# A gated attention kernel: chunks 1 to 5 in halves of 64 tokens, with one matmul for scores x v and q x state

## The chip, the core and the metric

The kernel runs on one core of a Trainium2 chip. A core has five engines that matter here, each with its own queue that it works off in order: TensorE (PE; its weight loads are listed as PEld), VectorE (DVE), ScalarE (ACT), GpSimd (POOL) and SyncE (SP), which issues nearly all transfers between device memory and the on-chip memory. TensorE writes its results to PSUM, from where ScalarE or VectorE fetch them. The metric is the device time of one execution in microseconds (us); lower is better.

## The reference

Two parts follow one another. The first is a gated linear attention, for 4 batches, 8 heads, 768 tokens and 48 features a head. It keeps a 48 x 48 state for each head:

```python
for t in range(S):
    state = alpha[:, :, t, :, None] * state + np.einsum('bhd,bhe->bhde', k[:, :, t], v[:, :, t])
    y[:, :, t] = np.einsum('bhd,bhde->bhe', q[:, :, t], state)
```

Its output is laid out as 4 x 768 rows of 384 values. The second part normalizes each row, multiplies it by a gain and sends it through two layers with a ReLU between them:

```python
xn = (x - mu) / np.sqrt(var + 1e-06) * g_ln
ch = np.maximum(xn @ w_ch1, 0.0) @ w_ch2
return (x + ch)
```

`w_ch1` is 384 x 1536 and `w_ch2` is 1536 x 384. Both arrive as 64-bit floats; the kernel turns them into 32-bit floats on the core.

## The kernel before

**Tiling.** The tokens are cut into 6 chunks of 128. `attention(c, b)` handles chunk c of batch b with tokens on the partitions: 24 blocks. Inside a chunk the recurrence is written with the running sum L of log alpha. `tri`, a triangle of ones, times log alpha gives L in PSUM (`lps`, line 249). ScalarE makes exp(-L) (`ek`, line 253) and exp(L) (`eq`, 254). GpSimd forms k x exp(-L) (line 256), VectorE q x exp(L) (258). TensorE transposes both (`tps`, 272), and ScalarE or VectorE copies them to `qkT` (276, 278). The scores are k against q, two heads at a time in the upper and lower half of the array (`aps`, 285); VectorE keeps the causal ones in `at` (289). The output `yps` is the sum of q x state (302, not in chunk 0) and scores x v (307). The state for the next chunk is the old one plus k x v (`sps`, 321; 326), times the gate exp(L) of the chunk's last token (331, on GpSimd). The gate goes from the last row of `eq` to a DRAM row (262) and back as columns (294). The output is stored (`kept`, 314), normalized (335 to 342), transposed (349) and copied to `xT` (351).

**The two layers.** `mlp()` takes chunk after chunk, with all four batches as columns. Chunk 0 is done directly (`hidden`, 372, and `project`, 384). Chunks 1 to 5 use a scheme with fewer products of combined blocks: `hidden_product` (612) and `product` (455). It needs sums of blocks of the operands: of w1 (`combine_first`, GpSimd, 565), of w2 (`combine_weights`, GpSimd, 415), of x (`combine_x`, VectorE, 588) and of the hidden values (`combine_hidden`, VectorE, 442). VectorE adds the products up (465, 468, 622 to 655), GpSimd does some late sums (471, 631 to 651), and ScalarE the ReLUs (664). `take_weights(i)` rounds one of 12 pieces of the weights, in three steps on VectorE, ScalarE and VectorE, and then starts the load of a later piece.

**What sets the order.** Every one of these functions yields after a few instructions, and the string `ORDER` says which takes the next turn: the letters a to x are the 24 attention blocks, A to L the pieces of weights, M the two layers, S the sums of the weights, R, X, N and O the ReLUs, sums and output loads. Each engine's queue is filled in the order of these turns.

**PSUM.** The pool has three tags: "a", three slots, for `lps`, `tps` and `aps`; "s", two slots, for `yps`, `sps` and `xps`; "m", three slots, for the two layers.

**Loads.** `load` brings one tensor of one chunk and batch in one transfer of 192 KB, on SP's queue. At the start alpha comes first, then k and q, then v, then three pieces of weights.

Of the kernel before, what the change touches and what calls it, by code (L numbers as in the profile page):

```python
# [25 lines left out]
    "babdabcdcabadcbacabbdabaabacababdabacbdbccbadAccdddcBcCedfeacbacaeBeffcgbaededbe"  # L26
    "eghfbAefgfcachfbdcheaaffbaefgdjBddeedbdcgfbeicCjgdfihcgjdCeAhccAgBDfghddEfeOgegi"
    "DfDeeiMfhMMMiMDMMiegMGEgEMMMOfeGghhigMMjhiCEfggFMhOGFHFgMGghMiHkfMMfiHeFIjhfHeMM"
    "IkJSIhhkhhlMMjIMfMglKJKjJLfgMljjLKLhhMSSMihSikMhOSgiMMSSMgShjkSjhiiMXjiSXSiXiXMk"
    "kMXkSllMXMXMlSMMXnMnMMkSMSMSiXmMSXMnMSMSMSMSjkMMkikjMXlMMMMMMRMllMMMljOMRSMMMSlk"  # L30
    "jlklMjjSRimMMnMSMjRMMMnMMMMkMnnmnMMMkMRMpjMMMnMRlMlllnmMmiRmOlMSmMRmMoMmmOMMJMRM"
    "SmSjmNSjlRMMRmoNinjkkNMmNMMkolMNRpoMlOKpMNMmMMMoMmoNmMNkNMMMNMMNMnMNqMkMNMMMopMM"
    "NSMMnolMoMlNpkNMoMMMOkOMMonnXXXXpMMXXMMXXXpoMMMMMMMMpXMMXMMoMMMrMMMMqMMMrMMMmnMM"
    "pRMomRnprmmMRqRopMMpMRMoMMmRmMMMMMrprnMnrnMMMoopppnMtpMqRMMMOMtrqMqnMMoMpqMprMRq"
    "RMMqNsMqMOMNRMNtrRnrMNMqMqqNMssRMMMNssoMMMNMNNMNsMMMNopMqqqqqrMMNMMsNtpMMNMMOprM"
    "MMNqsMqtMMooMMsNpMMXMMsMXXMstMqrrXtuXXXMtMMXXMMvMMMMXsvMMMtXMstMOrMMMMMMMMMvMMrr"
    "rsMtMvOsMMrtMMMMLuRMsMMvvMMMMMRRMtMrRMuMORvxMMMRRMstrMMstRqttsMqRuMsMMNRMuMRNMMN"
    "NMvMtuurvMxMMMMNsNtRtMMwNNvMMMsrMNMwMMNNMNMMwtNMMuMMuuMMMMMNuMwMNMMNwMMuttsxMMuv"
    "XXXvxMvuuXXXXxvwxMXMxxMMuwMXMwxMMXMMXMMMMMvMMwMwMxMMMRMuOwMuOMMwMMMMwuMMxwMwRMRM"
    "MxRMMRMvMMMMwxMMMMMMMMMuMMuMRMRRvMMMRNwxuRMMvMOMRxMMxvwMMNwMxNNMNxRNMMuxMMwMNMvM"  # L40
    "MONMwMNNMNMMMNwMMNMxMxMMvMMxwNMONMMNxMMMvMMXvOXXXMXXXMMMMMMXXMMMMMMMMXMMMMMRMXMM"
    "RMMMMMMMMMMMMMMMRRMMMMORMMMMMRMMMMRMMMMMMMMMRMRRMRMMNMMMNMMMNNNRMMNNMNMNMMMNNMMM"
    "ONMNMMMMMMMMMMMMMNNMMNMMMMMMM"
# [4 lines left out]
def kernel(  # L48
# [51 lines left out]
    raw = ctx.enter_context(tc.tile_pool(name="raw", bufs=B))  # L100
# [7 lines left out]

    r = np.arange(P)
    upto = (r[None, :] >= r[:, None]).astype(np.float32)  # L110
    const_np = np.concatenate([upto, np.eye(P, dtype=np.float32)], 1)
# [3 lines left out]
    def load(c, b, names="akqv"):  # L115
        for n, src in (("a", alpha), ("k", k), ("q", q), ("v", v)):
            if n not in names:
                continue
            t = raw.tile([P, H, D], FP32, name=f"r{n}", tag=f"r{n}",
                         bufs=B)  # L120
            nc.sync.dma_start(t, src[b, c * P:(c + 1) * P])
            raws[n, c, b] = t
# [5 lines left out]
    for names in ("a", "kq", "v"):  # L128
        for b in range(B):
            load(0, b, names)  # L130
# [4 lines left out]
    g_col, g20 = small[:, :NF], small[:, NF:2 * NF]  # L135
    eps, least = small[:, 2 * NF:2 * NF + 1], small[:, 2 * NF + 1:]
# [6 lines left out]
    for i in range(NJ // 2):  # L143
        cs, js = slice(2 * i * P, 2 * (i + 1) * P), slice(2 * i, 2 * (i + 1))
        pieces.append((w1[:, :, cs], w1_src[:, :, cs], True))
        pieces.append((w2[:, js], w2_src[:, js], False))
# [3 lines left out]
    def load_weights(i):  # L150
        if i >= len(pieces):
            return
        dst, src, _ = pieces[i]
        if src.dtype != FP32:
            dst = staged[i] = stage.tile(list(dst.shape), INT64, name="ws", tag="ws")
        nc.sync.dma_start(dst, src)

    def round_weights(i):
# [4 lines left out]
        dst, _, gains = pieces[i]  # L163
# [14 lines left out]
        if not gains:  # L178
            stt(out=dst, in0=dst, scalar=2.0 ** -20, in1=hi.bitcast(FP32),
                op0=AOP.mult, op1=AOP.mult)  # L180
            return
        for f in range(NF):
            stt(out=dst[:, f], in0=dst[:, f], scalar=g20[:, f:f + 1],
                in1=hi[:, f].bitcast(FP32), op0=AOP.mult, op1=AOP.mult)

    def take_weights(i):
        if pieces[i][1].dtype != FP32:
            yield from round_weights(i)
        elif pieces[i][2]:
            for f in range(NF):  # L190
                nc.vector.tensor_scalar_mul(pieces[i][0][:, f], pieces[i][0][:, f],
                                            g_col[:, f:f + 1])
        yield
        load_weights(i + STAGED)
        yield

    for i in range(STAGED):
        load_weights(i)
# [8 lines left out]
    eqs = [cpool.tile([P, NP, 2, 64], FP32, name=f"eq{b}") for b in range(2)]  # L207
    eqs += [shared[:, i * NP * P:(i + 1) * NP * P].rearrange(
        "p (a b c) -> p a b c", b=2, c=64) for i in range(2)]
    qks = [cpool.tile([P, 2, NP, 2, 64], FP32, name=f"qk{b}") for b in range(3)]  # L210
    qks.append(shared[:, 2 * NP * P:].rearrange("p (i a b c) -> p i a b c", i=2, b=2, c=64))
    sts = [cpool.tile([P, NP, 2, D], FP32, name=f"st{b}") for b in range(B)]
    for b in range(B):
        nc.vector.memset(eqs[b].rearrange("p a b c -> p (a b) c")[:, :, D:], 0.0)
        nc.vector.memset(qks[b].rearrange("p i a b c -> p (i a b) c")[:, :, D:], 0.0)
        nc.gpsimd.memset(sts[b], 0.0)
# [15 lines left out]
    ats = [cpool.tile([P, 2, NP, P], FP32, name=f"at{i}") for i in range(2)]  # L232
# [9 lines left out]
    def attention(c, b):  # L242
        qk = qk_of(c, b).rearrange("p i a b c -> p i (a b) c")
        eq = eq_of(c, b).rearrange("p a b c -> p (a b) c")[:, :, :D]
        la = work.tile([P, H, D], FP32, name="la", tag="la")
# [3 lines left out]
        nc.tensor.matmul(lps[:, :DM], tri, la, start=True, stop=True)  # L249
        yield  # L250
        lv = lps[:, :DM].rearrange("p (h d) -> p h d", d=D)
        ek = work.tile([P, H, D], FP32, name="ek", tag="ek")
        nc.scalar.activation(out=ek, in_=lv, func=AFT.Exp, scale=-1.0)
        nc.scalar.activation(out=eq, in_=lv, func=AFT.Exp)
        yield
        nc.gpsimd.tensor_mul(qk[:, 1, :, :D], raws.pop(("k", c, b)), ek)  # L256
        yield
        nc.vector.tensor_mul(qk[:, 0, :, :D], raws.pop(("q", c, b)), eq)
        if c + 1 < NCB:
            row = dram.tile([1, NP, P], FP32, name="row", tag="row")  # L260
            gate = work.tile([P, NP], FP32, name="gate", tag="gate", bufs=B)
            nc.sync.dma_start(row, eq_of(c, b)[P - 1:P].rearrange("o a b c -> o a (b c)"))
        yield
        n = c * B + b + (B if c < 2 else B // 2)
        if c < 2 or 3 * B <= n < NCB * B:
            load(*divmod(n, B), "akq")
        yield
        qkT = work.tile([R, 2, NP, P], FP32, name="qkT", tag="qkT", bufs=2)
        for i in range(2):
# [5 lines left out]
            if i == 0 or c < 2:  # L275
                nc.scalar.copy(out=qkT[:, i], in_=tps)  # L276
            else:
                nc.vector.tensor_copy(out=qkT[:, i], in_=tps)
            yield
        at = ats[b % len(ats)]  # L280
        aps = [ps.tile([P, NP, P], FP32, name=f"aps{i}", tag="a", bufs=3) for i in range(2)]
        for p in range(NP):
            for i in range(2):
                rows = slice(64 * i, 64 * i + D)
                nc.tensor.matmul(aps[i][:, p], qkT[rows, 1, p], qkT[rows, 0, p],  # L285
                                 start=True, stop=True)
        yield
        for i in range(2):
            nc.vector.copy_predicated(out=at[:, i], data=aps[i],  # L289
                                      mask=mask.unsqueeze(1).broadcast_to([P, NP, P]))  # L290
        yield
        if c + 1 < NCB:
            with nc.allow_non_contiguous_dma(reason="one row to columns"):
                nc.sync.dma_start(gate, row.rearrange("o a c -> c (o a)"))
        yield
        vt = raws.pop(("v", c, b))
        yps = ps.tile([P, NP, 2, D], FP32, name="yps", tag="s")
        sides = [slice(64 * s, 64 * s + 64) for s in range(2)]
        for p in range(NP):
            if c > 0:  # L300
                for s in sides:
                    nc.tensor.matmul(yps[s, p].rearrange("p a b -> p (a b)"), qkT[:, 0, p, s],  # L302
                                     sts[b][:R, p].rearrange("p a b -> p (a b)"),
                                     start=True, stop=False)
            for i in range(2):
                for s in sides:
                    nc.tensor.matmul(yps[s, p, i], at[:, i, p, s], vt[:, 2 * p + i],  # L307
                                     start=(c == 0), stop=(c == 0 or i == 1))
        yield
        x = work.tile([P, DM], FP32, name="x", tag="x", bufs=3)  # L310
        nc.scalar.copy(out=x, in_=yps.rearrange("p a b d -> p (a b d)"))
# [3 lines left out]
        yield  # L315
        if c + 1 < NCB:
            sps = ps.tile([R, NP, D], FP32, name="sps", tag="s")
# [407 lines left out]
```

## Time and profile before

| | |
|---|---|
| median of 3 runs | 476.17 us (473.99 to 476.75) |
| span of the profiled execution | 472.3 us |
| VectorE: scores kept, L289, x48 | 724 ns each |
| VectorE: q x exp(L), L258, x20 | 797 ns each |
| VectorE: copy of the transposed k, L278, x16 | 682 ns each |
| VectorE: normalization, L342, x24 | 587 ns each |
| GpSimd: k x exp(-L), L256, x22 (2 more in another tile) | 1059 ns each |
| GpSimd: state x gate, L331, x20 | 959 ns each |
| ScalarE: copies of the transposed q and k, L276, x32 | 597 ns each |
| ScalarE: exp(-L), L253, x24 | 490 ns each |
| HBM read and written | 33.20 and 9.48 MB |

The profile is of one execution, and its span runs from the first to the last instruction; what lies before and after it is part of the device time alone. The duration of an instruction is from its start to its end, and instructions of one engine overlap, so durations of one group can sum to more than the time it takes: where TensorE is meant, the distance from one start to the next is the better measure. An f32 matmul of the code shows as two matmul rows.

### The profile page before, as it was taken

How to read it: one execution, taken by the hardware profiler on the slowest of the kernel's cores; microseconds unless marked ns; L12 is line 12 of the kernel's file. 1: busy time of each engine (PE TensorE's matmuls, PEld its weight loads, DVE VectorE, ACT ScalarE, POOL GpSimd, SP SyncE). 2: the span in 40 equal slices, each digit the busy share in tenths (PEclk: the TensorE clock that was granted, in tenths of full speed). 3: DMA queues.
4: the chain of work that ended last, by engine and by line, in shares of the span. 5: the costliest groups of instructions: out<-in, count | busy, mean ns of one | idle time of the engine just before them, and what ended most of it. 6: DMA issues, size and time to landing. Idle time of an engine off the chain costs nothing.

```text
span 472.3 us, 9365 instructions
## 1 busy us (share of the span) xinstructions
PE 457.1 (97%) x3690; PEld 384.5 (81%) x3690; DVE 356.6 (76%) x662; ACT 152.9 (32%) x335; POOL 222.7 (47%) x222
## 2 busy tenths in 40 slices
PE   7899999999999999999999999999999999998996
PEld 5768465567688889998898998898998899987896
DVE  3799899867377799876788867688677579765673
ACT  4576354511033523124342121543031341223300
POOL 4142103069969990727461426460435360544513
PEclk9999999999999999999999999999999999999999
DMA  8986856403301422240331231330020110210001
GB/s 260 334 248 196 282 157 224 123 19 102 85 17 52 129 75 67 70 118 15 104 101 52 86 102 51 83 101 1 34 81 23 35 35 0 80 56 0 1 18 51
DMA packets 40132, 43.29 MB, mean 92 GB/s; under 512 B 13956, under 2 KB 36228, under 8 KB 40088
## 3 DMA queue, kind: packets, MB, share of 16 engines
q1 hardware_dynamic: 39544, 42.56, 29.4%
q8 instruction: 29, 0.48, 0.4%
q10 hardware_dynamic: 544, 0.13, 0.1%
q14 instruction: 15, 0.12, 0.1%
HBM read 33.20 MB, written 9.48 MB: 90 GB/s over the span
## 4 chain that ended last, share of the span: by engine, by line
PE 85%; DVE 5%; POOL 4%; ACT 2%; DMA 2%; issue 2%; POOLq 0%; DVEq 0%; ACTq 0%
PE ops L455 24%; PE hps L612 24%; PE hps L372 7%; PE ops L384 7%; PE aps L285 5%; PE yps L307 4%; PE tps L272 4%; PE yps L302 4%; PE lps L249 3%; PE sps L321 2%; PE xps L349 2%; DMA rk<-in_k_dram 1%; DVE at L289 1%; DVE sum L588 1%; DMA ra<-in_alpha_dram 1%
## 5 line engine op out<-in xcount | busy, mean ns | idle before, releaser
L471 POOL TENSOR_TENSOR ob<-ob,u 128x192 f32<-128x192 f32 x40 | 27.5, 699 | 83.3 <-DVE ob L468 63.9
L612 PE MATMUL hps<-sum,w 128*128 128x256 f32 x240 | 59.9, 382 | 1.1 <-DVE hT L655 1.1
L612 PEld LDWEIGHTS hps<-sum,w 128*128 128x128 f32 x240 | 44.7, 190 | 7.9 <-DVE hT L655 1.5
L455 PE MATMUL ops<-w,hT 128*128 128x192 f32 x280 | 49.6, 328 | 0.0
L664 ACT ACTIVATE hT<-hT 128x512 f32<-128x512 f32 x60 | 36.3, 628 | 35.6 <-POOL hT L634 21.3
L455 PEld LDWEIGHTS ops<-w,hT 128*128 128x128 f32 x280 | 45.7, 190 | 1.1
L331 POOL TENSOR_TENSOR st<-st,gate 128x384 f32<-128x384 f32 x20 | 19.1, 959 | 53.6 <-DVE st L326 44.3
L631 POOL TENSOR_TENSOR hT<-hT,u 128x512 f32<-128x512 f32 x10 | 12.9, 1287 | 56.9 <-DVE u L630 56.9
L256 POOL TENSOR_TENSOR qk<-rk,ek 128x384 f32<-128x384 f32 x22 | 23.3, 1059 | 30.0 <-PE sps L321 12.6
L307 PE MATMUL yps<-rv,at 128*64 128x48 f32 x768 | 36.5, 219 | 0.1
L289 DVE COPY_PREDICATED at<-consts,aps 128x512 f32<-128x512 int32 x48 | 32.2, 724 | 3.6 <-PE aps L285 3.2
L307 PEld LDWEIGHTS yps<-rv,at 128*64 128x64 f32 x768 | 32.9, 138 | 0.6 <-DVE at L289 0.3
L372 PE MATMUL hps<-xT,w 128*128 128x512 f32 x72 | 32.4, 597 | 0.0
L384 PE MATMUL ops<-w,hT 128*128 128x384 f32 x96 | 32.2, 488 | 0.0
L612 PE MATMUL hps<-xT,w 128*128 128x256 f32 x120 | 31.1, 382 | 0.9 <-DVE hT L644 0.9
L285 PE MATMUL aps<-qkT 48*128 48x128 f32 x384 | 28.6, 285 | 2.1 <-DVE at L289 1.3
L285 PEld LDWEIGHTS aps<-qkT 48*128 48x128 f32 x384 | 23.8, 187 | 8.0 <-issue 4.0
L302 PE MATMUL yps<-st,qkT 112*64 112x96 f32 x320 | 29.8, 257 | 0.0
L455 PE MATMUL ops<-ws,sum 128*128 128x192 f32 x160 | 28.9, 328 | 0.7 <-DVE sum L442 0.7
L455 PE MATMUL ops<-ws,hT 128*128 128x192 f32 x160 | 29.5, 327 | 0.0
L276 ACT COPY qkT<-tps 112x512 f32<-112x512 f32 x32 | 18.2, 597 | 29.0 <-PE tps L272 25.7
L455 PEld LDWEIGHTS ops<-ws,sum 128*128 128x128 f32 x160 | 26.3, 190 | 1.4 <-DVE sum L442 1.0
(141 smaller groups left out, 1020.9 us busy)
## 6 DMA issues: line engine op xcount, KB each, us to landing
ws<-in_moe_w_ch_dram SPq DMA_DIRECT2D x12, 768.0 KB, 6.1
ra<-in_alpha_dram SPq DMA_DIRECT2D x24, 192.0 KB, 2.6
rk<-in_k_dram SPq DMA_DIRECT2D x24, 192.0 KB, 3.4
rq<-in_q_dram SPq DMA_DIRECT2D x24, 192.0 KB
rv<-in_v_dram SPq DMA_DIRECT2D x24, 192.0 KB, 2.8
kept<-x SPq DMA_DIRECT2D x24, 192.0 KB, 1.9
ob<-kept SPq DMA_DIRECT2D x24, 192.0 KB, 2.9
out_dram<-ob SPq DMA_DIRECT2D x19, 192.0 KB, 1.9
```

The source lines that it names most:

```text
L256: nc.gpsimd.tensor_mul(qk[:, 1, :, :D], raws.pop(("k", c, b)), ek)
L285: nc.tensor.matmul(aps[i][:, p], qkT[rows, 1, p], qkT[rows, 0, p], start=True, stop=True)
L289: nc.vector.copy_predicated(out=at[:, i], data=aps[i], mask=mask.unsqueeze(1).broadcast_to([P, NP, P]))
L302: nc.tensor.matmul(yps[s, p].rearrange("p a b -> p (a b)"), qkT[:, 0, p, s], sts[b][:R, p].rearrange("p a b -> p (a b)"), start=True, stop ...
L307: nc.tensor.matmul(yps[s, p, i], at[:, i, p, s], vt[:, 2 * p + i], start=(c == 0), stop=(c == 0 or i == 1))
L331: nc.gpsimd.tensor_mul(st, st, gate.unsqueeze(2).broadcast_to([P, NP, 2 * D]))
L372: nc.tensor.matmul(hps, w1[:, f, j * P:(j + 1) * P], xT_of[c][:, f], start=(f == 0), stop=(f == NF - 1))
L384: nc.tensor.matmul(ops_of[b], hT_of[c][:, j, b], w2[:, j], start=(j == 0), stop=(j == NJ - 1))
L455: nc.tensor.matmul(acc, lhs[:, j], rhs[:, j], start=(j == 0), stop=(j == NT - 1))
L471: getattr(nc.gpsimd, f"tensor_{op}")(x, x, y)
L612: nc.tensor.matmul(acc[:, i], w, b, start=True, stop=True)
L664: nc.scalar.activation(out=x, in_=x, func=AFT.Relu)
```

## The change

Chunk 0 stays in one piece of 128 tokens. In chunks 1 to 5 the chunk is worked in two halves of 64: `tri2` is a triangle in each half, so L starts again at token 64. The scores of a half are 64 x 64, so a block of scores takes only half of the partitions of `at`. The other half holds the transposed q of the same head and half, and the matching partitions of the new tile `va` hold the state beside v: one matmul over both (line 399 of the new kernel) gives scores x v plus q x state, so that the separate one is gone. For this the state has to be copied into `va` (`carry`, on ScalarE, two copies for each half), and q's transposed copy goes straight into `at` in two copies. The state is brought forward twice a chunk, in halves (`ups`, line 372), each with a VectorE add and a GpSimd product with the gate. In chunk 5, too, the first half does so.

Further: exp(-L) is written back to PSUM over L, and VectorE, not GpSimd, multiplies it with k. `eq` has the four pairs of heads innermost, so that a gate is read back in pieces of 16 bytes. Copies of the transposed k are ScalarE's after chunk 0 and VectorE's in chunk 0. From chunk 2 on the normalization is ScalarE's, with one tiny product on VectorE. The sums of w2 go from GpSimd to VectorE. Alpha, k and q are loaded for two batches at a time; v in six transfers for two batches, as its parts go to different partitions. One piece of weights is queued ahead of k and q at the start. `ORDER` is new throughout, with W as the letter for the sums of w2.

```diff
-        ek = work.tile([P, H, D], FP32, name="ek", tag="ek")
-        nc.scalar.activation(out=ek, in_=lv, func=AFT.Exp, scale=-1.0)
         nc.scalar.activation(out=eq, in_=lv, func=AFT.Exp)
+        nc.scalar.activation(out=lv, in_=lv, func=AFT.Exp, scale=-1.0)
         yield
-        nc.gpsimd.tensor_mul(qk[:, 1, :, :D], raws.pop(("k", c, b)), ek)
+        nc.vector.tensor_mul(qk[:, 1], raws.pop(("k", c, b)), lv)
...
+            if i:
+                (nc.vector.tensor_copy if whole else nc.scalar.copy)(out=kT, in_=tv)
+            elif whole:
+                nc.scalar.copy(out=qT, in_=tps)
+            else:
+                for j in range(2):
+                    nc.scalar.copy(out=at[rows[j], :, j], in_=tv[rows[j]])
...
+                for s in range(2):
+                    nc.tensor.matmul(aps[i][halves[1 - i], p, s], kT[rs, p, s], at[rs, p, i, s],
+                                     start=True, stop=True)
...
+        ups = [ps.tile([R, NP, D], FP32, name=f"ups{s}", tag="s")
+               for s in range(1 if last or whole else 2)]
+        for p in range(NP):
+            for s, up in enumerate(ups):
+                for i, h in enumerate(heads):
+                    ts = slice(0, P) if whole else halves[s]
+                    vs = va[:, 0, i, p] if whole else rv[ts, p] if s == i else va[ts, s, i, p]
+                    nc.tensor.matmul(up[h, p], qk_of(c, b)[ts, 1, p, i, :h.stop - h.start],
+                                     vs, start=True, stop=True)
+        yield
+        st = sts[b]
+        def carry(s, to):
+            for i, h in enumerate(heads):
+                nc.scalar.copy(out=to[h, s, i], in_=st[h])
+        for s, up in enumerate(ups):
+            by = gate[:R, s].unsqueeze(2).broadcast_to([R, NP, D])
+            if whole:
+                nc.vector.tensor_mul(st, up, by)
+                yield
+                continue
+            nc.vector.tensor_add(st, up, st)
+            yield
+            nc.gpsimd.tensor_mul(st, st, by)
+            yield
+            if s == 0:
+                carry(1, va)
+                yield
...
-            if c > 0:
-                for s in sides:
-                    nc.tensor.matmul(yps[s, p].rearrange("p a b -> p (a b)"), qkT[:, 0, p, s],
-                                     sts[b][:R, p].rearrange("p a b -> p (a b)"),
-                                     start=True, stop=False)
             for i in range(2):
-                for s in sides:
-                    nc.tensor.matmul(yps[s, p, i], at[:, i, p, s], vt[:, 2 * p + i],
-                                     start=(c == 0), stop=(c == 0 or i == 1))
+                rs = slice(0, P if whole or i == 0 else R)
+                for s in range(2):
+                    nc.tensor.matmul(yps[halves[s], i, p], at[rs, p, i, s],
+                                     va[rs, 0 if whole else s, i, p], start=True, stop=True)
...
+        if not last:
+            carry(0, raws["v", c + 1, b][1])
...
-        add, sub = nc.gpsimd.tensor_add, nc.gpsimd.tensor_sub
+        add, sub = nc.vector.tensor_add, nc.vector.tensor_sub
         ready = win["b"] = {4: b[4], 7: b[1], 11: b[4], 14: b[2], 15: b[2], 17: b[0]}
```

## The prediction

> **What bounds the kernel now.** I read the page's engine totals and the totals of the chain of waits first, then TensorE's timeline, since both point at it.
>
> ```profile
> PE 457.1 (97%) x3690; PEld 384.5 (81%) x3690; DVE 356.6 (76%) x662; ACT 152.9 (32%) x335; POOL 222.7 (47%) x222
> PE 85%; DVE 5%; POOL 4%; ACT 2%; DMA 2%; issue 2%; POOLq 0%; DVEq 0%; ACTq 0%
> ```
>
> TensorE is occupied for nearly the whole span. So what counts is how long its queue takes, read from one start to the next (durations overlap). One attention block of a chunk after the first, one of chunk 0, a state product, and two `lps` pairs:
>
> ```profile
> 199.55 1.16 PE L285 MATMUL aps<-qkT 48*128 48x128 f32 x16
> 200.64 0.39 PE L302 MATMUL yps<-st,qkT 112*64 112x96 f32 x4
> 200.86 0.39 PE L307 MATMUL yps<-rv,at 128*64 128x48 f32 x8
> ...
> 202.38 1.57 PE L455 MATMUL ops<-w,hT 128*128 128x192 f32 x8
> ...
> 33.62 1.14 PE L307 MATMUL yps<-rv,at 128*64 128x48 f32 x32
> 34.69 0.55 PE L349 MATMUL xps<-consts,xn 128*128 128x128 f32 x3
> ...
> 45.59 0.63 PE L321 MATMUL sps<-rv,qk 128*64 128x48 f32 x16
> 46.15 1.16 PE L285 MATMUL aps<-qkT 48*128 48x128 f32 x16
> ...
> 79.40 0.81 PE L249 MATMUL lps<-la,consts 128*128 128x384 f32 x2
> 80.14 0.39 PE L302 MATMUL yps<-st,qkT 112*64 112x96 f32 x4
> ...
> 87.91 0.81 PE L249 MATMUL lps<-la,consts 128*128 128x384 f32 x2
> 88.56 0.60 PE L272 MATMUL tps<-consts,qk 128*112 128x128 f32 x4
> ```
>
> Each f32 matmul of the code is two rows here. Read: scores (`aps`) take 200.64 - 199.55 = 1.09 us for 16 rows; q x state and scores x v together 202.38 - 200.64 = 1.74; scores x v alone, in chunk 0, 34.69 - 33.62 = 1.07; the state product 46.15 - 45.59 = 0.56. An `lps` pair takes 0.65 when a full-array transpose follows (87.91 to 88.56) and 0.74 when a matmul on part of the array follows (79.40 to 80.14): a change of array shape costs 0.09.
>
> VectorE is second. The stretches cut at the first hidden-layer matmul (47.2) and the first projection (89.0) show where it is tight:
>
> ```profile
> 0.00:47.20 47.20, 40.62 (x522) 31.90 (x522) 35.79 (x72) 28.48 (x65) 16.44 (x23) 1.00 0.84 259
> 47.20:89.00 41.80, 41.80 (x265) 22.62 (x263) 38.94 (x64) 18.62 (x36) 6.73 (x7) 1.00 0.65 206
> 126.40:300.00 173.60, 172.75 (x1541) 155.30 (x1540) 136.87 (x250) 53.56 (x122) 101.04 (x86) 1.00 0.27 76
> ```
>
> The columns after the length are PE, PEld, DVE, ACT, POOL, clock, DMA share, GB/s. From 47 to 89 us VectorE has 2.9 us free of 41.8; in the long middle 37 of 174.
>
> [...]16 rows of 128 columns in 1.09 us are 0.068 a row, while full-array transposes of 128 columns take 0.11 (four from 88.56 to 89.00), and the change of shape cost 0.09.[...] the q product (L258) takes 0.53 to 1.39 us for one shape, and the long ones lie beside GpSimd work at 9 to 13 us.[...]
>
> **The change, part by part** (against the profiled span, 472.3).
>
> 1. *q x state leaves TensorE.* The L302 rows go in 20 blocks (chunks 1 to 5). What remains should cost what L307 costs alone: 1.74 - 1.07 = 0.67 each, -13.4 us.
>
> 2. *State products in halves.* 16 rows become 32, each with 64 of the contracted partitions, in chunks 1 to 4 (16 blocks); in chunk 5, which had none, 16 rows (4 blocks). If all four 64x64 tiles run side by side, 32 rows cost the present 0.56; if only two do, 1.12. I take 0.75: 16 x 0.19 = +3.0, and 4 x 0.56 = +2.2. Together +5.2; ends +2.2 and +11.2.
>
> 3. *Scores in halves.* 16 rows of 128x128 become 32 of 64x64, in two of the four tiles. Side by side they take the same 1.09; one after the other, at half of the transpose's 0.11, 32 x 0.055 = 1.76. The code now issues both halves of one tile before the other, but in the trace the rows of two tiles already run ahead of each other (single L302 rows start before the last L321 row at 63.7), so I take 1.15: 20 x 0.06 = +1.2; ends 0 and +13.4.
>
> 4. *Shape changes*: in the two issue orders I count 84 before and 89 after: 5 x 0.09 = +0.5.
>
> Sum for TensorE: -13.4 + 5.2 + 1.2 + 0.5 = -6.5.
>
> 5. *VectorE, GpSimd, ScalarE.* VectorE gets k x exp(-L), 24 times, reading PSUM; nearest row, the L388 add of one PSUM and one SBUF operand of 384 columns: 0.558, so +13.4. It gets the 13 sums of w2 (24.9 us of L415 on GpSimd; by the 512-column adds' 0.69 scaled to 768, 1.0 each): +13. It loses 16 copies L278 (0.68) but gets 4 in chunk 0: -8.2; loses 16 of 24 `xn` (0.587) for tiny products: -8.5; its state adds stay 40 of about 0.36. Net +10, less than its free 116 us, and less contention, as GpSimd gives up 50 us. ScalarE gets 80 carry copies (0.32 by the 192-column copies: +26), two score copies for one in 20 blocks, and 16 `xn`; it stays under half the span. These sums lie beside TensorE's work. What can show is the tight stretch: with the prices above, VectorE's queue ahead of the first hidden matmul falls from about 40 to 34 us, but from there to the first projection it grows from 37 to 45 (eight pieces of weights begun instead of seven, nine finished instead of six), against 42 us of TensorE work. So VectorE leads there by about 2 us. And k's product now sits behind weight rounding in VectorE's queue, with `lps`' slot and the transposes waiting for it. Scores x v now also waits for VectorE's add, GpSimd's gate product (0.83 for twice its size now, L331) and two carry copies (0.64); whatever follows it on TensorE waits too, but other blocks and hidden matmuls are queued between, as far as the order lists them. I take +1.5 for all this; ends -1 (the earlier first hidden matmul) and +6.
>
> 6. *DMAs.* Loads go in pairs of 384 KB; one 768 KB piece of weights is put on SP's queue ahead of k and q. By the rate of the first 12 us (261 GB/s, the issue starting at 0.7 us) alpha and that piece are 1.5 MB, k's first pair lands near 8 to 9 us; exp(-L) is ready at 9.2 in the present trace (L253 ends there), so it costs at most about 1 us, inside item 5. v becomes six queue entries a pair of batches where it was two, in pieces of 768 bytes, while alpha, k and q become three where they were six; after 89 us the DMA share is 0.22 to 0.27, so nothing. Gates move in 128 or 256 pieces in place of 512: nothing, they lie ahead of need. In chunk 5 four more gates: nothing.
>
> 7. *The end.* The last 28 us keep their order (products, GpSimd's `late` sums, sends): 0.
>
> Sum: -6.5 + 1.5 = -5.0; span 467.3. The median of the runs lies 3.9 above the profiled span (476.17 - 472.3), so 471.2.
>
> **The rivals.**
>
> A, *tiles do not overlap as hoped*: items 2 and 3 at their dear ends: -13.4 + 11.2 + 13.4 + 0.5 + 1.5 = +13.2, 489.4. For: the order of halves within a tile; two PSUM tiles of one block. Against: L285 and L321 already overlap.
>
> B, *slower by VectorE's hold on PSUM*: with ek gone, the `lps` slot (tag a, three slots for `lps`, `tps`, `aps`) is freed by VectorE's product and not by ScalarE's exp, and the two `ups` hold both slots of tag s until VectorE adds them. TensorE, being in order, then stops, with hidden and output matmuls queued behind. For: 93% VectorE in 47 to 89 us. Against: 79% in the middle. It decides once waits exceed 6.5 us, 0.33 us in each of 20 blocks; it is slower beyond noise from 0.45. At 0.7, 14 us: 472.3 - 6.5 + 14 = 479.8, 483.7.
>
> C, *no change*: VectorE's stretch at its dear end: -6.5 + 6 = 471.8, 475.7.
>
> D, *more gain*: cheap ends: -13.4 + 2.2 + 0 + 0.5 and a start 3 us earlier (5.5 us less TensorE work is queued ahead of the first hidden matmul): -13.7, 462.5.
>
> **How the numbers follow.** Forecast 0.48, A 0.10, B 0.16, C 0.13, D 0.13. 0.5% is 2.4 us, what a measurement here can tell. Faster: D and nearly all of the forecast, 0.59; within: C and the forecast's edge, 0.15; slower: A and B, 0.26. The range leaves out A, half of B and the tail of D: 462 to 483. The forecast alone is 467 to 474.
>
> **What would show it.** The new L399 near 1.07 us a block, `ups` 0.56 to 0.8, `aps` about 1.1; fewer than 5 us of TensorE idle before VectorE releases from 47 to 89 us. Wrong if `aps` is near 1.8 or `ups` near 1.1 (A), or if the waits' view has TensorE waiting for VectorE or for `lps`, `ups` slots by over 8 us (B).

## The result, and the profile after

| | before | changed |
|---|---|---|
| median of the runs | 475.13 us (473.99 to 476.75) | 482.21 us (481.37 to 483.79) |
| span of the profiled execution | 472.3 us | 479.7 us |
| mean clock of TensorE in it | 1.000 | 0.989 |

The ratio is 1.0155, with a 95% interval of 1.0118 to 1.0192: the change costs about 7 us where the forecast had it gain 5. The page's engine totals and the totals of the chain of waits, for the changed kernel:

```profile
PE 454.8 (95%) x4010; PEld 377.1 (79%) x4010; DVE 366.5 (76%) x687; ACT 219.8 (46%) x463; POOL 177.6 (37%) x199
PE 54%; DVE 23%; POOL 8%; DMA 5%; ACT 5%; issue 4%; SPq 0%; POOLq 0%; DVEq 0%; ACTq 0%
```

TensorE's part of the chain fell from 85% to 54%, and VectorE's rose from 5% to 23%. TensorE's own busy time is no longer than it was (454.8 us against 457.1); something keeps it waiting. One full attention block on TensorE's timeline of the changed kernel (the rows in the middle are single rows of the state product and the scores, started in turn):

```profile
206.38 1.14 PE L399 MATMUL yps<-va,at 128*64 128x48 f32 x32
207.45 1.02 PE L345 MATMUL aps<-at,kT 48*64 48x64 f32 x27
208.26 0.25 PE L372 MATMUL ups<-rv,qk 64*64 64x48 f32 x1
...
208.82 0.28 PE L372 MATMUL ups<-va,qk 64*64 64x48 f32 x2
209.03 0.59 PE L545 MATMUL ops<-w,hT 128*128 128x192 f32 x2
```

From 206.38 to 209.03 the block takes 2.65 us. The same block of the kernel before, from its own timeline:

```profile
218.99 0.39 PE L302 MATMUL yps<-st,qkT 112*64 112x96 f32 x4
...
220.63 0.63 PE L321 MATMUL sps<-rv,qk 128*64 128x48 f32 x16
221.19 1.16 PE L285 MATMUL aps<-qkT 48*128 48x128 f32 x16
222.28 0.70 PE L612 MATMUL hps<-xT,rq 128*128 128x256 f32 x2
```

It took 222.28 - 218.99 = 3.29, so this block is 0.64 us shorter. Over all 20 blocks of chunks 1 to 5, counted in the traces from each row's start to the next row's with idle time left out, the rows of the output, the scores and the state product take 64.4 us before and 54.9 after. So the change does what it says on TensorE, with -9.5 us, and the changed kernel loses some 17 us elsewhere. The waits of TensorE by what ended them (us in total, times, longest), the changed kernel:

```profile
PE xps L439 <- DVE xn L427: 3.9, 3, 3.3
PE lps L253 <- DVE more L250: 2.8, 1, 2.8
PE yps L399 <- ACT va L379: 2.4, 2, 2.0
PE lps L288 <- ACT la L285: 1.3, 1, 1.3
PE tps L323 <- DVE qk L294: 1.2, 1, 1.2
```

All lines of this view sum to 20.1 us, against 11.1 in the kernel before, where the normalized x was waited for in all for

```profile
PE xps L349 <- DVE xn L342: 0.2, 1, 0.2
```

The second line (2.8 us) is the start and is the same in both. The first is nearly all new, one wait of 3.3 us. Most of the rest that is new lies before 75 us: the carry copy `va`, log alpha, and k's product.

The last part of the loss is the clock. Three stretches of the changed kernel, the three before them, with the columns as in the windows shown earlier (PE, PEld, DVE, ACT, POOL, clock, DMA share, GB/s):

```profile
12.00:15.40 3.40, 3.38 (x10) 2.00 (x10) 2.80 (x5) 3.40 (x7) 0.00 (x0) 0.50 1.04 358
70.00:73.40 3.40, 3.40 (x53) 2.41 (x49) 3.33 (x6) 0.86 (x2) 1.72 (x1) 0.50 0.67 229
114.40:117.80 3.40, 2.91 (x7) 2.00 (x8) 3.40 (x6) 1.77 (x5) 0.22 (x1) 0.50 0.27 89
...
8.60:12.00 3.40, 1.43 (x4) 0.30 (x2) 2.97 (x5) 2.40 (x5) 0.00 (x0) 1.00 1.06 385
66.60:70.00 3.40, 1.92 (x51) 1.74 (x53) 3.37 (x7) 2.30 (x5) 1.98 (x2) 1.00 0.42 125
111.00:114.40 3.40, 0.58 (x4) 0.25 (x2) 3.40 (x1) 0.00 (x0) 3.40 (x6) 1.00 0.53 142
```

In each of the first three TensorE was granted 0.50 of its clock, and in the 3.4 us ahead of it TensorE had worked only 0.58 to 1.92 us. As an estimate from these rows, 3.4 us at 0.50 cost at most 1.7 us, so three cost at most 5.1. The kernel before keeps the full clock from 8.4 us on in its profiled execution, but not in most others: of 32 executions timed beside the first experiments, 12 were granted 0.999 or 1.000 and took 472.8 to 474.8 us, and 20 were granted 0.992 to 0.995 and took 475.3 to 476.8. At 0.993, where both kernels have executions, the kernel before takes 476.62 (median) and the changed one 481.37 (one execution). So the clock explains less between the medians than between the two profiles.

The sum, from the two profiles: -9.5 (rows of the attention blocks) + 9.7 (TensorE's idle time: 479.7 - 454.8 = 24.9 after, 472.3 - 457.1 = 15.2 before) + 7.3 (all other rows of TensorE, the same matmuls in both kernels, counted as above: 392.3 before, 399.6 after) = +7.5, where the span shows 479.7 - 472.3 = +7.4. The waits' view names 9.0 of the 9.7 (20.1 - 11.1). Of the 7.3 the clock can explain at most 5.1, and the changes of shape were forecast at 0.5 but not measured by themselves; the remaining 1.7 or more aren't assigned.

### The profile page after: what moved, and what is told of

It is laid out like the page before. It is cut to its first block, busy times and chain, and to the rows that moved or that the text cites. A ratio compares the mean times of both kernels' runs of the same rounds, so it can differ in the third digit from the quotient of the medians.

```text
span 479.7 us, 10173 instructions
## 1 busy us (share of the span) xinstructions
PE 454.8 (95%) x4010; PEld 377.1 (79%) x4010; DVE 366.5 (76%) x687; ACT 219.8 (46%) x463; POOL 177.6 (37%) x199
## 4 chain that ended last, share of the span: by engine, by line
PE 54%; DVE 23%; POOL 8%; DMA 5%; ACT 5%; issue 4%; SPq 0%; POOLq 0%; DVEq 0%; ACTq 0%
PE ops L545 20%; PE hps L702 18%; DMA ws<-in_moe_w_ch_dram 5%; PE ops L474 3%; PE aps L345 3%; PE yps L399 2%; PE tps L323 2%; DVE w L205 2%; PE lps L288 2%; DVE at L356 2%; DVE sum L678 2%; DVE qk L296 2%; DVE ws L211 2%; DVE sum L532 2%; PE ups L372 1%
## 5 line engine op out<-in xcount | busy, mean ns | idle before, releaser
L389 POOL TENSOR_TENSOR st<-st,gate 112x192 f32<-112x192 f32 x36 | 27.3, 762 | 129.1 <-DVE st L387 99.8
L561 POOL TENSOR_TENSOR ob<-ob,u 128x192 f32<-128x192 f32 x40 | 25.5, 647 | 73.7 <-DVE ob L558 52.0
L545 PEld LDWEIGHTS ops<-w,hT 128*128 128x128 f32 x280 | 45.6, 190 | 0.7 <-DVE ob L555 0.2
L379 ACT COPY va<-st 64x192 f32<-64x192 f32 x80 | 27.9, 348 | 27.3 <-POOL st L389 26.5
L356 DVE COPY_PREDICATED at<-consts,aps 64x512 f32<-64x512 int32 x40 | 29.2, 731 | 10.7 <-PE aps L345 9.5
L399 PEld LDWEIGHTS yps<-va,at 128*64 128x64 f32 (+1 forms) x768 | 24.9, 137 | 10.5 <-issue 5.6
L399 PE MATMUL yps<-va,at 128*64 128x48 f32 (+1 forms) x768 | 28.3, 224 | 2.7 <-ACT va L379 2.4
L323 PE MATMUL tps<-consts,qk 128*112 128x128 f32 x176 | 26.9, 283 | 1.8 <-DVE qk L294 1.2
L333 ACT COPY at<-tps 64x512 f32<-64x512 f32 (+1 forms) x40 | 23.1, 578 | 11.5 <-PE tps L323 7.5
L474 PEld LDWEIGHTS ops<-w,hT 128*128 128x128 f32 x96 | 18.5, 198 | 11.9 <-issue 0.9
L323 PEld LDWEIGHTS tps<-consts,qk 128*112 128x112 f32 x176 | 20.4, 137 | 8.1 <-DVE qk L294 2.1
```

The lines of the kernel that those rows point to most:

```text
L323: nc.tensor.transpose(tps[:, p], qk_of(c, b)[:, i, p].rearrange("p a b -> p (a b)")[:, :R], ident)
L333: nc.scalar.copy(out=at[rows[j], :, j], in_=tv[rows[j]])
L356: nc.vector.copy_predicated(out=at[h, :, i], data=aps[i][h], mask=mask[h, h].unsqueeze(1).unsqueeze(1).broadcast_to([HS, NP, 2, HS]))
L379: nc.scalar.copy(out=to[h, s, i], in_=st[h])
L389: nc.gpsimd.tensor_mul(st, st, by)
L399: nc.tensor.matmul(yps[halves[s], i, p], at[rs, p, i, s], va[rs, 0 if whole else s, i, p], start=True, stop=True)
```

## The experiments

The theories. S: the new layout of `eq` makes ScalarE's exp and VectorE's q product slower. H: a run of GpSimd's sums holds a VectorE instruction that TensorE needs. O: the piece of weights put ahead of k and q opens the pauses of the first 20 us. K: k's product in VectorE's queue does. L, the plain rival to H: VectorE simply has too much to do. All kernels were timed in five rounds beside the kernel before, whose median there was 475.3 to 475.6. As the granted clock differs from execution to execution of one kernel, medians are also compared below between executions with the same mean clock, where there are some.

### The layout of eq

What speaks for S in the traces, minimum, median and maximum in ns, the kernel before first, then the changed one:

```profile
L254 ACT ACTIVATE eq<-lps x20: 477/485/524, 9.1 to 344.2; 128x384 f32<-128x384 f32 x20
L258 DVE TENSOR_TENSOR qk<-rq,eq x20: 528/592/1387, 9.6 to 349.5; 128x384 f32<-128x384 f32 x20
```

```profile
L291 ACT ACTIVATE eq<-lps x20: 852/878/905, 8.3 to 341.0; 128x384 f32<-128x384 f32 x20
L296 DVE TENSOR_TENSOR qk<-rq,eq x20: 835/852/1926, 11.9 to 359.6; 128x384 f32<-128x384 f32 x20
```

Same elements, and 0.39 us more for the exp, 0.26 to 0.31 for the product (median, minimum). The prediction priced both at no change. The first experiment keeps the changed kernel and makes `eq` contiguous (gates are then read back in 4-byte pieces):

```diff
-    eqs = [cpool.tile([P, 2, 64, NP], FP32, name=f"eq{b}") for b in range(2)]
+    eqs = [cpool.tile([P, NP, 2, 64], FP32, name=f"eq{b}") for b in range(2)]
...
-        eq = eq_of(c, b).rearrange("t i c p -> t i p c")[:, :, :, :D]
+        eq = eq_of(c, b).rearrange("t p i c -> t i p c")[:, :, :, :D]
...
-            nc.sync.dma_start(gate[:, :ne], row[:ne].rearrange("o (r p) -> r o p", p=NP))
+            nc.sync.dma_start(gate[:, :ne], row[:ne].rearrange("o (p r) -> r o p", p=NP))
```

> The changed kernel with exp(L) laid out contiguously again; gates are read back in 4-byte pieces. Theory S (the 16-byte step of eq costs engine time that TensorE ends up waiting for): the q product falls from 0.85 to about 0.55 us and the exp from 0.88 to 0.49; 24 of each are 7 us of VectorE and 9 us of ScalarE, most of it in the stretch where VectorE is full, so 3 to 7 us off the time (475 to 479). Theory O (the order of VectorE's queue decides, with its waits for weights and its place behind weight rounding): the same two durations fall, the time by less than 1.5 us.

Measured: 477.52 us, ratio 1.0046 (1.0030 to 1.0062), so 4.7 us of the 7.1 are gone. At a clock of 0.989 the median is 477.64 against 481.50 for the changed kernel, at 0.993 477.23 against 481.37, so the gain isn't a matter of the clock alone. The two rows in this kernel:

```profile
L291 ACT ACTIVATE eq<-lps x20: 468/490/515, 7.3 to 337.1; 128x384 f32<-128x384 f32 x20
L296 DVE TENSOR_TENSOR qk<-rq,eq x20: 524/552/1618, 11.8 to 355.7; 128x384 f32<-128x384 f32 x20
```

The reverse test takes the kernel before and gives it only the new step of `eq` (and with it gates in 16-byte pieces):

```diff
-    eqs = [cpool.tile([P, NP, 2, 64], FP32, name=f"eq{b}") for b in range(2)]
+    eqs = [cpool.tile([P, 2, 64, NP], FP32, name=f"eq{b}") for b in range(2)]
...
-        eq = eq_of(c, b).rearrange("p a b c -> p (a b) c")[:, :, :D]
+        eq = eq_of(c, b).rearrange("p b c a -> p a b c")[:, :, :, :D]
```

> The kernel before with only the new layout of eq (step of 16 bytes for exp and q product, gates in 16-byte pieces). Theory S: q product and exp get longer by 0.3 and 0.4 us each, and the time rises by 2 to 5 us. Theory O: the old order has enough slack, the time changes by less than 1.5 us.

Measured: 477.57 us, ratio 1.0067 (1.0041 to 1.0092); the exp has a median of 885 ns, the q product of 914. S holds in both directions. By the medians the step costs 2.2 us in the kernel before, but 8 of these 11 executions were granted 0.998 or 0.999, more than the kernel before mostly gets. At the same clock it costs 3.1 to 4.6 us (477.57 against 473.01 at 0.999, 478.44 against 475.37 at 0.995, 481.14 against 476.62 at 0.993), about as much as in the changed kernel. The pieces in which gates are read back change along in both experiments and weren't tried apart.

### GpSimd's run at 110 us

The changed kernel at TensorE's longest wait; GpSimd, VectorE and TensorE from their timelines:

```profile
110.49 4.12 POOL L655 TENSOR_TENSOR w<-w 128x384 f32<-128x384 f32 x6
...
106.95 0.47 DVE L427 TENSOR_SCALAR xn<-x,mv,rstd 128x384 f32<-128x384 f32 x1
...
110.83 4.01 DVE L427 TENSOR_SCALAR xn<-x,mv,rstd 128x384 f32<-128x384 f32 x1 [1.56 <-ACT rstd L423]
...
114.89 0.90 PE L439 MATMUL xps<-consts,xn 128*128 128x128 f32 x3 [3.31 <-DVE xn L427]
```

The same instruction takes 0.47 us at 106.95 and 4.01 at 110.83. It starts just after GpSimd's run of six sums has begun and ends at 114.84, just after the run does (110.49 + 4.12 = 114.61). The first attempt moved this normalization to ScalarE, but left a product of one column on VectorE (its expectation calls H "P"):

```diff
-        if c < 2:
+        if c < 1:
             nc.vector.tensor_scalar(out=xn, in0=x, scalar1=mv[:, 0:1], scalar2=rstd[:, :1],
```

> The changed kernel with the normalization of chunk 1 on ScalarE too (it is VectorE's in chunks 0 and 1). Theory P (a VectorE instruction[...] waits until a run of GpSimd instructions ends; one such took 4.0 us and TensorE stood still 3.5 us for it): that gap at 111 us is gone and the time falls by 3 to 5 us, to 477 to 479. If the 4 us were an accident of one execution: no change within 1 us.

Measured: 483.41 us, ratio 1.0183 (1.0148 to 1.0218), no gain. VectorE's timeline says why:

```profile
110.89 3.29 DVE L430 SCALAR_TENSOR_TENSOR rstd<-mv,rstd 128x1 f32<-128x1 f32 x1 [1.94 <-ACT rstd L423]
```

A product of one column took 3.29 us beside the same run; TensorE stood 3.71 us for what follows from it. So an instruction of one column was held too: the same product takes 0.15 us at 106.59 in this kernel. The next kernel, on contiguous `eq`, takes both away from VectorE in chunk 1:

```diff
-        if c < 2:
+        if c == 0:
...
+        elif c == 1:
+            shift = rstd[:, 1:]
+            nc.scalar.activation(out=shift, in_=mv[:, 0:1], func=AFT.Identity, scale=rstd[:, :1])
+            nc.scalar.activation(out=shift, in_=shift, func=AFT.Identity, scale=-1.0)
+            nc.scalar.activation(out=xn, in_=x, func=AFT.Identity, scale=rstd[:, :1], bias=shift)
```

> The contiguous-eq kernel (477.5 us), with the whole normalization of chunk 1 on ScalarE[...]. Theory H (the hold by GpSimd's run is what stops TensorE there, and costs it a window of half clock besides): no TensorE gap above 1 us at 105 to 115, one half-clock window less, 472 to 474. Rival (another held instruction, the hidden-layer sums or the output adds, makes TensorE wait there instead): a gap stays, 476.5 to 478.

Measured: 475.88 us, ratio 1.0024 (1.0007 to 1.0041). That is 1.6 us below contiguous `eq` alone, but the two intervals overlap, and the wait only moved: VectorE's two sums of weights were held next,

```profile
107.34 7.31 DVE L510 TENSOR_TENSOR ws<-w 128x768 f32<-128x768 f32 x2
```

They took 7.31 us, where two take 1.81 at 114.76 us in the changed kernel, and TensorE still stood 2.96 us, now for the statistics behind them. That is the rival's outcome, by H's mechanism. Then GpSimd was given more work, the 13 sums of w2 (again on contiguous `eq`):

```diff
-        add, sub = nc.vector.tensor_add, nc.vector.tensor_sub
+        add, sub = nc.gpsimd.tensor_add, nc.gpsimd.tensor_sub
         ready = win["b"] = {4: b[4], 7: b[1], 11: b[4], 14: b[2], 15: b[2], 17: b[0]}
```

> The contiguous-eq kernel (477.5 us), with the 13 sums of w2 back on GpSimd. Theory L (VectorE's load is the bound in the stretch from 47 to 120 us): VectorE is about 13 us lighter, 474 to 476. Theory H (GpSimd's back-to-back runs are what hold VectorE): 13 to 25 us more of GpSimd's work beside VectorE's, more held instructions, 477.5 to 480.

Measured: 481.34 us, ratio 1.0131 (1.0103 to 1.0160), 3.8 us worse with a lighter VectorE. L is wrong in sign, and the hold grew:

```profile
108.41 5.57 DVE L427 TENSOR_SCALAR xn<-x,mv,rstd 128x384 f32<-128x384 f32 x1 [1.47 <-ACT rstd L423]
```

It met a run of four sums of w2 (7.09 us from 105.72) and was let in shortly after these had ended, while GpSimd went on with its sums without a pause to 119.35; a second normalization took 2.61 at 117.36. TensorE's waits for `xn` are 5.4 us against 4.3 with contiguous `eq` alone. That isn't the whole loss: another 2.1 us went at 171 us, for ScalarE, which had stood behind GpSimd's gate product.

The direct test leaves the normalization where it was and takes the run itself off GpSimd, on contiguous `eq`. Its expectation speaks of three sums; the condition catches four of the 17, as two of the sums write `a[4]` and two write `a[5]` (each sum is two instructions, and the trace has eight of them on VectorE, from 124.0 to 133.2). Three of the four are the run at 110 us:

```diff
-                op(out[i], x[i], y[i])
+                on = nc.vector if out is a[4] or out is a[5] else nc.gpsimd
+                (on.tensor_add if op is add else on.tensor_sub)(out[i], x[i], y[i])
```

> The contiguous-eq kernel (477.5 us) with only the three first sums of w1 on VectorE, chunk 1's normalization as in the changed kernel. Theory H, with the hold as the only cause of the gap at 109 to 113 us: 472.5 to 474, as with ScalarE's normalization (472.8). Rival (VectorE's normalization is late there by its own queue): a wait above 1.5 us of TensorE for xn stays, 475 to 477.

Measured: 472.96 us, ratio 0.9950 (0.9933 to 0.9967): 4.6 us less than with contiguous `eq` alone, and 2.5 less than the kernel before. At a clock of 0.993 the medians are 473.44 here, 477.23 with contiguous `eq` alone and 476.59 for the kernel before, so neither difference is a matter of the clock alone. The normalization and TensorE's next step, in this kernel:

```profile
109.69 0.48 DVE L427 TENSOR_SCALAR xn<-x,mv,rstd 128x384 f32<-128x384 f32 x1 [1.46 <-ACT rstd L423]
...
110.05 0.82 PE L439 MATMUL xps<-consts,xn 128*128 128x128 f32 x6
```

There is no hold and no wait, and the stretches at half clock near 112 us, two of them in the kernel with contiguous `eq` alone (111.9 to 118.7), are gone. The same edit together with the normalization on ScalarE:

> The kernel with contiguous eq and ScalarE's normalization in chunk 1 (475.9 us), with three of GpSimd's 17 first sums of w1, the six back-to-back products of 128x384 and 128x128 at about 109 us, on VectorE. Theory H (GpSimd's back-to-back run holds whichever VectorE instruction meets it): no VectorE instruction of 3 us or more between 105 and 120 us, TensorE's gap of 2.96 us there gone, 473 to 474.5. Rival (VectorE is late there by its own load, the hold only fills its slack): the gap stays above 2 us, 475.5 to 477.

Measured: 472.77 us, ratio 0.9951 (0.9933 to 0.9969). Not to be told from the edit alone, so the ScalarE normalization adds nothing once the run is gone. And with all 17 sums on VectorE (`add, sub = nc.vector.tensor_add, nc.vector.tensor_sub` there), again together with ScalarE's normalization:

> The same kernel with all 17 first sums of w1 on VectorE (about 17 x 0.75 = 12.8 us more of it between 100 and 130 us). Theory H: no held instruction at all there, and if VectorE has room, 473 to 475. Theory L (VectorE's load sets the stretch to 130 us): a longer wait of TensorE for VectorE, 477 to 482.

Measured: 479.37 us, ratio 1.0077 (1.0048 to 1.0107), 6.6 us more than with four. The hold is gone here too, but TensorE now waits at 130 us, for a copy, and at 135 us, for one of these sums in VectorE's longer queue,

```profile
PE aps L345 <- ACT kT L328: 2.7, 2, 2.3
PE hps L707 <- DVE rq L660: 2.5, 1, 2.5
```

and it is slower from 130 us on: two score rows take 0.37 us at 131.25 against 0.22 at 118.47, with a mean clock of 0.986 in this execution. So both hold, each in its place: one run of GpSimd's sums costs more than it saves, and all 17 on VectorE are too many for it.

### The start

On the changed kernel, the first rounding of the early piece of weights was put later in the order, its load left where it was:

```diff
-    "bbBBaddbcccaaaabbdccadabbcbbaaaabdacbbbcccbAcfcaabddddadbeBA
+    "bbBaddbcccaaaabbdccadabbcbbaaaabdacbbbcccbAcfcaabddddadbeBBA
```

> The changed kernel with the first VectorE step of the first piece of weights moved in the order from ahead of the first k and q products to just before the ScalarE step of the same piece; its load stays first. Theory O: VectorE's first k product starts near 9.3 in place of 11.4 us[...], and the first hidden-layer matmul comes 2 to 4 us earlier; the time falls by 2 to 4 us, to 478 to 480. Rival: VectorE is full until the projections anyway, so the work moved comes back later and the time changes by less than 1 us.

Measured: 485.27 us, ratio 1.0225 (1.0184 to 1.0266), a miss. k still arrives behind the piece (k's first product starts at 10.1 in place of 11.4), and the work put off collides later: in the profiled execution, the slowest of six (490.06, mean clock 0.972), TensorE runs at half clock in five stretches, 27 us in all. Then, on contiguous `eq`, both the load and the rounding went behind chunk 0's k, q and v:

```diff
-    "bbBBaddbcccaaaabbdccadabbcbbaaaabdacbbbcccbAcfcaabddddadbeBAbfffeeAgaeeaaccccdbb"
+    "bbaddbcccaaaaBbbdccadabbcbbaaaabdacbbbcccbAcfcaabddddadbeBBAbfffeeAgaeeaaccccdbb"
```

> The contiguous-eq kernel (477.5 us), with the piece of weights loaded and rounded after chunk 0's k, q and v in place of ahead of them. Theory O (the piece ahead of k and q delays VectorE's first k product and so opens the gaps of the first 20 us, which cost a window of half clock): first k product near 9.2 us, no half clock between 8 and 20 us, 473.5 to 475.5. Rival (the start is hidden behind hidden-layer matmuls whatever its order): 476.5 to 478.5.

Measured: 477.99 us, ratio 1.0059 (1.0038 to 1.0079), no gain. The first k product does start at 9.20 us, as O asked, and in the profiled execution (479.83, among the slowest of 16, mean clock 0.982) the clock falls near 28.7 us (0.99 from 25.3 to 28.7, with TensorE busy for 2.15 us); by an estimate from the mean clock, 17 us in all are at half clock. Together with ScalarE's normalization:

> Both edits together on the contiguous-eq kernel. Theories H and O: their gains add, 468 to 471, below the kernel before (475.3). If either rival holds, 472 to 477.

Measured: 476.97 us, ratio 1.0036 (1.0021 to 1.0051), again nothing over the normalization alone (475.88), although no half clock at all falls in its profiled execution (mean clock 0.999). By these times O falls; where the start's gain goes isn't settled. Last, k's product back on GpSimd (contiguous `eq`, exp(-L) into SBUF):

```diff
-        la = work.tile([P, 2, NP, D], FP32, name="la", tag="la")
+        la = work.tile([P, 2, NP, D], FP32, name="la", tag="la", bufs=3)
...
-        nc.scalar.activation(out=lv, in_=lv, func=AFT.Exp, scale=-1.0)
+        nc.scalar.activation(out=la, in_=lv, func=AFT.Exp, scale=-1.0)
         yield
-        nc.vector.tensor_mul(qk[:, 1], raws.pop(("k", c, b)), lv)
+        nc.gpsimd.tensor_mul(qk[:, 1], raws.pop(("k", c, b)), la)
```

> The contiguous-eq kernel (477.5 us) with k x exp(-L) back on GpSimd, exp(-L) written to SBUF by ScalarE in place of log alpha (three slots for it). Theory K (k's product in VectorE's queue is what makes TensorE wait in the first 60 us): VectorE 13 us lighter, TensorE's gaps before 60 us fall from 9.9 to about 7 us, 474 to 476. Rival (GpSimd's longer work, 1.0 us a product beside VectorE's, gives it back): 477 to 480.

Measured: 476.14 us, ratio 1.0014 (0.9995 to 1.0032). That is 1.4 us less than with contiguous `eq` alone, and the two intervals just touch (1.0032 and 1.0030). It isn't for K's reason: the early waits grew, the longest of them being now

```profile
PE lps L288 <- ACT la L285: 4.2, 1, 4.2
...
PE aps L345 <- ACT at L333: 2.5, 1, 2.5
```

while the wait for `xn` at 110 us is gone. The normalization isn't held in this kernel:

```profile
112.23 0.60 DVE L427 TENSOR_SCALAR xn<-x,mv,rstd 128x384 f32<-128x384 f32 x1 [1.43 <-ACT rstd L423]
```

VectorE's next two sums of weights take 2.88 us at 112.76, where two take 1.82 at 120.47. What lets the normalization in here isn't known. So it isn't shown that moving this product to VectorE costs anything; whether the third slot for log alpha or its longer hold made the 4.2 us was not tried.

## Why the prediction was wrong

- Step 1 (q x state leaves TensorE) was right in kind and somewhat too large: scores x v with the carry takes 1.07 us a block (206.38 to 207.45), and over chunks 1 to 5 the rows of the output fell from 33.9 to 22.5 us, -11.5 where -13.4 was taken.
- Steps 2 and 3 were too dear: scores and state products rose from 30.5 to 32.5 us, +2.0 where +6.4 was taken. In the block shown they take 2.65 - 1.07 = 1.58 us, less than the 1.65 before (1.09 + 0.56), so the rows on different parts of the array (the prediction's tiles) overlap near the cheap end. With step 4 as forecast TensorE gains about 9 us, not 6.5. Rival A is out.
- Step 5 failed: +1.5 us, with +6 as its dear end, stood for VectorE, GpSimd and ScalarE; about 16 us (7.4 + 9.0) came. Several totals in it were right: VectorE's busy time rose by 9.9 (forecast 10), GpSimd's fell by 45 (forecast 50), and VectorE is 44.3 us busy between the first hidden matmul and the first projection (forecast 45). That the first of these fits is partly luck: the q products cost 3.8 us more in all and the normalization saved 2.5 in place of 8.5, while the sums of the hidden values and of x came 11 us cheaper (63.5 to 57.7 and 32.5 to 27.3), which had no number in the forecast. What failed is what was concluded from totals, in two terms:
  - The q product and the exp were carried over at their old price; that the step of 16 bytes costs nothing was the author's assumption, shown by no run. The measured price is 0.26 to 0.31 us for a product on VectorE (there are 24) and 0.39 for an exp (24 too). Undoing the step gave 4.7 us. A step that no run had shown should have had a dear end in the range, and it had none.
  - "Less contention, as GpSimd gives up 50 us" took contention for something that goes with GpSimd's total alone; the 11 us of cheaper sums fit that, and one run outweighed it. In the trace of the changed kernel VectorE's normalization stood for 4.01 us, until the whole back-to-back run of six was over. This run, of 4.12 us, which the kernel before has too (4.92 us there), now met an instruction that TensorE needed. Undoing it gave 4.6 us.
- The clock had no place in the prediction. The full clock in the profile of before was taken as given, and three stretches at half clock after pauses of 1.3 to 3.3 us cost up to 1.7 us each by the estimate above. It also hides in the 3.9 us that were added to the span: every execution's time lies about 1.8 above its own span (481.50 and 479.7), so the profiled execution took 474.1, and the other 2.1 are the distance of a full-clock execution from the median.
- Step 6 was right that the early piece of weights costs little: taking it away gave nothing. (Alpha, k and q come in pairs in chunks 0 to 2 only: the trace has 6 loads of 384 KB and 12 of 192 KB of each.)
- Rival B named nearly the measured time, 483.7, but by another way, so that its nearness is chance. Waits for `lps`' slot or behind k's product are 0.7 and 1.2 us in the waits' view, 1.9 together where 14 were worked out, and none is for the slots of `ups`; k's product off VectorE didn't shorten the early waits.

With both terms undone the kernel runs at 472.96 us, 2.5 below the kernel before, where the forecast had 471.2. TensorE's gain of 9 us is still spent in part before 60 us, where pauses for VectorE and, in the profiled execution, two stretches of half clock (12.0 to 15.4 and 22.2 to 25.6) remain. What would turn these into time isn't settled: no try on the start did.

## What to carry to other kernels

Taking work from the leading engine pays only as far as the others can keep it fed; look through the new order for the one instruction that it will wait for, and at what that instruction can collide with, not at busy totals. Keep operands that VectorE and ScalarE touch often contiguous: here a step of 16 bytes cost 0.39 us an exp and 0.26 to 0.31 a product, and a small transfer could carry the stride instead. Don't leave long back-to-back runs on GpSimd where VectorE has an instruction on the critical path: here moving four sums of 17 was worth 4.6 us, moving all 17 cost more than it gave. And before comparing two profiles, look at the clock of the other executions: one profile of a kernel can be a lucky one.

## What the runs showed of the hardware

- A step of 16 bytes between f32 elements: the exp of 384 columns goes from 0.485 us in the kernel before to 0.878 in the changed one (median), the product from 0.53 to 0.84 (minimum); with contiguous `eq` in the changed kernel they are 0.490 and 0.52.
- A VectorE instruction beside a back-to-back run of GpSimd sums stood through several of them: 4.01 us (384 columns, one input; changed kernel), 3.29 (one column; chunk 1's normalization on ScalarE but for this product), 6.44 (768 columns, two inputs; the whole normalization on ScalarE), each to about the end of the run (the first two ended at 114.84 and 114.18 us, the run beside them at 114.61 and 114.16; the third and the sum beside it at 114.65, the run at 112.97); 5.57 us beside the sums of w2, where it was let in before GpSimd's sums ended. In the kernel before VectorE and GpSimd took turns instead (4.92 us for the run in place of 4.12, VectorE's sums 0.42 to 1.12). With k's product on GpSimd the normalization took 0.60 us. What decides isn't known from these runs.
- In the profiled execution of the changed kernel the clock that TensorE was granted was 0.50 in three stretches of 3.41 us, from 11.97, 70.00 and 114.37 us, and 1.00 in the rest from 8.55 to 479.59 us; from one start to the next it is 58.03 and 44.37 us, 17 and 13 times 3.41. In the 3.4 us ahead of each, TensorE was busy for 1.43, 1.92 and 0.58 us. With four sums off GpSimd it was 1.68 and 2.42 us ahead of the two stretches at 0.50 (from 12.0 and 22.2 us). Similar busy times were also followed by the full clock: 2.14 us in the changed kernel (35.86 to 39.27), 2.42 in the kernel before (13.6 to 17.0). So in these stretches the busy time just ahead doesn't decide by itself. With ScalarE's normalization in chunk 1, a pause of 2.96 us, to 118.18 us, passed at a clock of 1.00 (100 to 126 us).
